# Emptying the finished banks first at a change of tile, in a convolution with two feed-forward layers

## The chip, the cores and the metric

The kernel runs on one core of a Trainium2 chip. The metric is the device time of one execution in microseconds (us). The kernel before takes 2165.09 us (median of three runs, 2159.32 to 2166.94).

## What is computed

The reference, cut to what matters:

```python
def _attn_ref(x, weight):            # x: 4 x 4096 x 192, weight: 8 x 7
    w = softmax(weight)              # seven taps for each of eight groups of 24 channels
    out = np.einsum('hk,bskhg->bshg', w, x_unf)   # causal convolution along the sequence
def _moe_ref(x, w_in, w_out):        # 16384 x 192, 192 x 2048, 2048 x 192
    r = np.maximum(x @ w_in, 0.0)
    return (r * r) @ w_out
def _moe2_ref(x, w_in, w_out):
    h = x @ w_in
    return np.maximum(0.01 * h, h) @ w_out
```

The output is `_moe2_ref(_moe_ref(_attn_ref(x)))`, in float32. A float32 operand is split into a high and a low part in a shorter format (`fp32r`), and a product is the sum of products of parts.

## The kernel before

**Tiles and steps.** The 16384 tokens are cut into 32 tiles of 512 (`TT`). A tile passes through layer 1 (squared ReLU) and layer 2 (leaky ReLU). Behind a start with two pairs of tiles, the tiles follow one by one: layer 1 of an even tile t, layer 1 of t + 1, layer 2 of t, layer 2 of t + 1, and so on (`phases`). These four are called here **1e, 1o, 2e and 2o**, and the four together a round. Each tile takes eight steps (`NP`), and a step handles two blocks of 128 of the 2048 hidden values; 512 steps are written out by one Python loop (`for s in range(NS)`), which sets the order of the instructions on each engine by hand. `tc.manual_schedule()` keeps that order.

**What a step does.** TensorE computes the first product `h` of a step (`g1`, 18 matmuls on halves of the rows, that is nine pairs that run side by side) and, two steps later (`LAG`), the second product (`g2_one`, nine pairs too). Between them, in the step's own turn:

- `act`: ScalarE applies the ReLU to the two `h` tiles into `g` (L576 in layer 1, L578 in layer 2).
- `square` (layer 1 only): one `g` is squared on VectorE (L583), the other on ScalarE (L585).
- `high`: ScalarE casts `g` to `hi` (L603), twice.
- `low`: VectorE subtracts, `lo` = `g` - `hi` (L607), twice.
- `add_low`: VectorE adds the two `lo` into `both` (L619). The second product takes `hi`, `lo` and, for one of its banks, `both`.
- `pieces`: other work that a budget places into the steps: the taps of the convolution for tiles to come (L433, L435, result `acc_a` or `acc_b`), the transposes of the input (L411), the splits of a finished layer 1 tile into the input of layer 2 (L475 on ScalarE, L484 on VectorE), and the transposes and stores of a finished layer 2 tile (L763, L768). At most `many` pieces go into one step, 2 in most.

**The change of tile.** A second product sums over the eight steps of a tile in three banks of PSUM, `M`, `F` and `E` (the tags `o0m`, `o1m`, `o0r`, `o1r` take turns as their names, and the fourth is free for the next tile's first bank). When the last one has been issued, `evac_one` empties the banks with functions that the step calls:

- `early` (ScalarE): L743 and L744 copy the two halves of bank E
- `other` (ScalarE): L747 copies one half of bank F
- `add_rest` (VectorE): L750 adds the other half of F and a copy of E
- `add_main` (VectorE): L753 adds bank M and the copies

The next tile's second product needs E's bank from its first third on, and F's from its second third on. TensorE issues in a step: five pairs of `h`, a third of the second product (three pairs), two pairs of `h`, the second third, two pairs of `h`, the last third. At the change the step of the next tile with p = 1 is the one in which the copies stand; `leaving` holds them, and `alone` says that a single tile is leaving. In the kernel before, `early` stands at the head of that step, `other` and `add_rest` behind the step's activations, its piece and its squares, and `add_main` at its end. The built program makes L750 wait for L747. For a pair of tiles `evac` has six functions (`take`, `shift`, `add`; L835, L840, L844), called at the end of the step.

The first 16 steps follow a written-out table (`ROW`, `play`) and are not touched.

Of the kernel before, what the change touches and what calls it, by code (L numbers as in the profile page):

```python
# [23 lines left out]
LAG = 2  # L24
# [39 lines left out]
def conv_moe_moe2_kernel(  # L64
# [16 lines left out]
    NP = NF // 2  # L81
# [221 lines left out]
    in_pair = {u for z in phases if len(z) == 2 for u in z}  # L303
# [428 lines left out]
    def evac_one(u):  # L732
# [25 lines left out]
        else:  # L758
# [21 lines left out]
            elif t % 2:  # L780
                then.append((700, rest, None, None))
        return (early, other, add_rest, add_main), then

# [18 lines left out]
    def evac_last(u):  # L802

        l, t = u
        (early, other, add_rest, add_main), _ = evac_one(u)
        early()
        other()
        add_rest()
        add_main()
        v = halves(t % 2)  # L810
# [14 lines left out]
    def evac(u):  # L825
# [7 lines left out]
        def take(i):  # L833
            z[i] = ring[:, i, :]
            (nc.vector.tensor_copy if i else nc.scalar.copy)(out=z[i], in_=o[i, "m"])  # L835
# [9 lines left out]

        now = [(0, lambda: take(0)), (690, lambda: take(1))]
        for i in range(2):
            now += [(0, lambda i=i: shift(i)), (690, lambda i=i: add(i))]
        if l == 1:
# [20 lines left out]
    with tc.manual_schedule():  # L870
# [285 lines left out]
        prep_next = 2  # L1156
        late = []
        left_at = -2
        going = begin_g1(0)
        for s in range(NS):  # L1160
# [45 lines left out]
            many = MANY[l - 1] + (l == 1 and s >= 4 * NP or 2 * NP - 4 <= s < 2 * NP) if s > 1 else 4  # L1206
            if left_at == s - 1:
                many = 1
# [3 lines left out]
            if s < 2 * NP:  # L1212
                play(s, A, Z)
                late = [Z]
                if s == 0:
                    split_a((1, 2), third)
                    split_a_lo((1, 2), third)
                continue
            if leaving:
                while leave:  # L1220
                    z = leave.popleft()
                    z[2]()
                    release()
                    budget[0] -= max(z[1], 0)
                while dec and getattr(dec[0][2], "second", False):
                    decode_one()
                if alone:
                    leaving[0]()
            left = [many, 1]
            if u in in_pair:  # L1230
                act(*A)
                if late and late[0] not in hi:
                    high(*late[0])
                if not alone:
                    needed(s, 10000)
                    pieces(s, left)
                while leaving and not alone and dec and getattr(dec[0][2], "second", False):
                    decode_one()
                if l == 1:
                    square(*A, False)  # L1240
                if alone:
                    leaving[1]()
                    leaving[2]()
                    leaving[3]()
                    needed(s, 10000)
                    pieces(s, left)
                if late:
# [5 lines left out]
            else:  # L1253
# [7 lines left out]
                needed(s, 10000)  # L1261
                if not (alone and dec):
                    pieces(s, left, 700)
                if l == 1:
                    square(*Z, vector)
                    square(*A, False)
                if alone:
                    leaving[1]()
                    leaving[2]()
                pieces(s, left)  # L1270
                while leaving and not alone and dec and getattr(dec[0][2], "second", False):
                    decode_one()
                high(*one)
# [3 lines left out]
                if three:  # L1277
                    add_low(u, p)
                if alone:
                    leaving[3]()  # L1280
                    budget[0] -= 1400
            if leaving and not alone:
                for c, fn in leaving:
                    fn()
                    budget[0] -= c
            release()
# [42 lines left out]
```

## Time and profile before

| | |
|---|---|
| median of three runs | 2165.09 us |
| the profiled execution, its own time | 2162.51 us |
| its span, first to last instruction | 2160.8 us |
| mean granted TensorE clock | 0.995 |
| TensorE matmul / weight load busy | 2084.4 / 1974.9 us |
| VectorE / ScalarE busy | 1648.7 / 1478.4 us |

The span is what the trace covers; the execution's own time is 1.7 us longer. PE is TensorE's matmuls, PEld its weight loads, DVE is VectorE, ACT is ScalarE. "idle before" of an instruction is the time its engine stood empty ahead of it, with what ended that time. Matmuls overlap, so busy time of PE is not work at full rate.

### The profile page before, as it was taken

How to read it: one execution, taken by the hardware profiler on the slowest of the kernel's cores; microseconds unless marked ns; L12 is line 12 of the kernel's file. 1: busy time of each engine (PE TensorE's matmuls, PEld its weight loads, DVE VectorE, ACT ScalarE, POOL GpSimd, SP SyncE). 2: the span in 40 equal slices, each digit the busy share in tenths (PEclk: the TensorE clock that was granted, in tenths of full speed). 3: DMA queues.
4: the chain of work that ended last, by engine and by line, in shares of the span. 5: the costliest groups of instructions: out<-in, count | busy, mean ns of one | idle time of the engine just before them, and what ended most of it. 6: DMA issues, size and time to landing. Idle time of an engine off the chain costs nothing.

```text
span 2160.8 us, 47005 instructions
## 1 busy us (share of the span) xinstructions
PE 2084.4 (96%) x18592; PEld 1974.9 (91%) x18592; DVE 1648.7 (76%) x2575; ACT 1478.4 (68%) x2700; POOL 60.1 (3%) x114
## 2 busy tenths in 40 slices
PE   9899999999999999999999999999999999999998
PEld 6789998999999899998999999999998999989997
DVE  8877678787787877778777787877778777787664
ACT  7877567667676666767667676676767667677674
POOL 2201110000000000000000000000000000000000
PEclk9999999999999999999999999999999999999999
DMA  8540131121212112131121211212121121311110
GB/s 191 137 108 21 27 54 26 39 37 45 37 24 46 29 45 40 21 65 26 36 38 32 50 26 38 37 44 38 24 50 26 45 41 21 64 26 35 25 31 16
DMA packets 232677, 95.07 MB, mean 44 GB/s; under 512 B 203208, under 2 KB 218696, under 8 KB 232456
## 3 DMA queue, kind: packets, MB, share of 16 engines
q1 hardware_dynamic: 229288, 88.90, 21.0%
q0 software_dynamic: 1168, 2.75, 0.6%
q8 instruction: 145, 2.38, 0.5%
q14 instruction: 76, 0.62, 0.1%
q10 hardware_dynamic: 2000, 0.42, 0.1%
HBM read 25.19 MB, written 12.58 MB: 17 GB/s over the span
## 4 chain that ended last, share of the span: by engine, by line
PE 65%; DVE 17%; ACT 11%; issue 5%; DMA 1%; SPq 0%; DVEq 0%; ACTq 0%
PE h L544 31%; PE o1m L544 12%; PE o0r L544 11%; PE o1r L544 7%; DVE lo L607 5%; PE o0m L544 4%; ACT hi L603 2%; DVE g L583 2%; DVE acc_b L435 2%; DVE ring L750 2%; ACT g L576 2%; DVE acc_a L435 2%; ACT ring L747 2%; ACT zs L744 2%; ACT g L578 2%
## 5 line engine op out<-in xcount | busy, mean ns | idle before, releaser
L544 PE MATMUL h<-x,w 64*128 64x512 f32 x9216 | 1362.9, 377 | 2.6 <-ACT g L578 1.4
L544 PEld LDWEIGHTS h<-x,w 64*128 64x128 f32 x9216 | 1067.5, 186 | 13.8 <-ACT g L578 1.8
L607 DVE TENSOR_TENSOR lo<-g,hi 128x512 fp32r<-128x512 f32 x1022 | 661.8, 688 | 347.1 <-ACT hi L603 289.7
L603 ACT CAST hi<-g 128x512 fp32r<-128x512 f32 x1020 | 580.9, 619 | 134.5 <-DVE g L583 130.8
L544 PE MATMUL o1m<-hi,w 64*128 64x512 f32 x2044 | 632.6, 385 | 30.5 <-DVE ring L750 28.7
L544 PE MATMUL o0r<-hi,w 64*128 64x512 f32 x1948 | 601.6, 384 | 17.9 <-DVE ring L750 17.9
L578 ACT ACTIVATE g<-h 128x512 f32<-128x512 f32 x512 | 279.6, 595 | 321.3 <-PE h L544 320.5
L544 PEld LDWEIGHTS o1m<-hi,w 64*128 64x128 f32 x2044 | 358.5, 186 | 59.9 <-DVE ring L750 37.7
L544 PEld LDWEIGHTS o0r<-hi,w 64*128 64x128 f32 x1948 | 342.2, 186 | 47.6 <-DVE ring L750 26.2
L544 PE MATMUL o0r<-lo,w 64*128 64x512 f32 (+1 forms) x1022 | 383.5, 378 | 0.4 <-DVE lo L607 0.4
L576 ACT ACTIVATE g<-h 128x512 f32<-128x512 f32 x512 | 278.6, 593 | 139.9 <-PE h L544 138.1
L544 PE MATMUL o1m<-both,w 64*128 64x512 f32 x926 | 352.4, 381 | 8.1 <-DVE both L619 8.1
L619 DVE TENSOR_TENSOR both<-lo 128x512 fp32r<-128x512 f32 x463 | 320.5, 692 | 18.0
L544 PE MATMUL o0m<-hi,w 64*128 64x512 f32 x1088 | 326.9, 380 | 4.4 <-ACT ring L835 3.2
L544 PE MATMUL o1r<-hi,w 64*128 64x512 f32 x1052 | 321.2, 380 | 1.0 <-ACT zs L744 1.0
L544 PE MATMUL o0m<-lo,w 64*128 64x512 f32 x560 | 209.1, 378 | 0.6 <-DVE lo L607 0.5
L544 PEld LDWEIGHTS o0m<-hi,w 64*128 64x128 f32 x1088 | 191.2, 186 | 9.7 <-ACT ring L835 4.0
L544 PE MATMUL o1r<-lo,w 64*128 64x512 f32 (+1 forms) x526 | 198.0, 376 | 0.0
L544 PEld LDWEIGHTS o1m<-both,w 64*128 64x128 f32 x926 | 172.3, 186 | 19.0 <-DVE both L619 16.8
L544 PEld LDWEIGHTS o0r<-lo,w 64*128 64x128 f32 (+1 forms) x1022 | 187.4, 183 | 2.3 <-issue 0.8
L544 PEld LDWEIGHTS o1r<-hi,w 64*128 64x128 f32 x1052 | 186.6, 186 | 2.4 <-ACT zs L744 1.4
L583 DVE TENSOR_TENSOR g<-g 128x512 f32<-128x512 f32 x243 | 165.6, 682 | 20.1 <-ACT g L576 17.4
(136 smaller groups left out, 1337.6 us busy)
## 6 DMA issues: line engine op xcount, KB each, us to landing
x<-x SPq DMA_DIRECT2D x189, 256.0 KB
out_dram<-y SPq DMA_DIRECT2D x186, 64.0 KB
raw_a<-in_x_dram SPq DMA_DIRECT2D x127, 64.0 KB
raw_b<-in_x_dram SPq DMA_DIRECT2D x62, 64.0 KB
lent<-in_moe_w_out_dram SPq DMA_DIRECT2D x13, 256.0 KB
lent<-in_moe_w_in_dram SPq DMA_DIRECT2D x13, 192.0 KB
lent<-in_moe_w_in_dram SPq DMA_DIRECT2D x13, 128.0 KB
lent<-in_moe_w_out_dram SPq DMA_DIRECT2D x13, 128.0 KB
```

What stands on the lines that cost most here:

```text
L435: nc.vector.scalar_tensor_tensor(out=acc[0], in0=src, scalar=w, in1=acc[0], op0=ALU.mult, op1=ALU.add)
L544: return nc.tensor.matmul(out=o.rearrange("p (b a) -> p b a", a=2), lhsT=w, rhs=z.rearrange("p (a b) -> p b a", a=2), start=begin, stop=end_,)
L576: nc.scalar.activation(out=g, in_=hps.pop((u, f)), func=ACTF.Relu)
L578: nc.scalar.activation(out=g, in_=hps.pop((u, f)), func=ACTF.Prelu, alpha=0.01)
L583: nc.vector.tensor_mul(out=g, in0=g, in1=g)
L603: nc.scalar.copy(out=a, in_=gsp[u, f])
L607: nc.vector.tensor_sub(out=b, in0=gsp.pop((u, f)), in1=f32(hi[u, f]))
L619: nc.vector.tensor_add(out=c, in0=f32(lo[u, 2 * p]), in1=f32(lo[u, 2 * p + 1]))
L744: nc.scalar.copy(out=got["s"][v], in_=E[w])
L747: nc.scalar.copy(out=z3[v], in_=F[w])
L750: nc.vector.tensor_add(out=zr[v], in0=F[v], in1=got["s"][v])
```

## The change

For a single tile, the three copies and the addition that frees bank F (`early`, `other`, `add_rest`) are called together at the head of the step; the pending low parts' sum of the step before (`add_low`, if `soon` said that a change follows) comes right behind them, then activations, squares, at most one piece, the casts and subtractions, and at the end `add_main`. For a pair, all six functions go to the head. The step of a change and the one behind it take one piece each at most; other pieces go to later steps.

```diff
--- before.py
+++ after.py
@@ -779,7 +779,7 @@
                 then.append((700, rest_alone, None, None))
             elif t % 2:
                 then.append((700, rest, None, None))
-        return (early, other, add_rest, add_main), then
+        return (early, other, add_rest), [add_main] + then
 
     ys = {}
 
@@ -802,11 +802,11 @@
     def evac_last(u):
 
         l, t = u
-        (early, other, add_rest, add_main), _ = evac_one(u)
+        (early, other, add_rest), then = evac_one(u)
         early()
         other()
         add_rest()
-        add_main()
+        then[0]()
         v = halves(t % 2)
         z, zr = ring[:, 0, :], ring[:, 2, :]
         dmas = [nc.sync, nc.scalar]
@@ -843,9 +843,7 @@
             v = halves(i)
             nc.vector.tensor_add(out=z["r"][v], in0=o[i, "r"][v], in1=z["s"][v])
 
-        now = [(0, lambda: take(0)), (690, lambda: take(1))]
-        for i in range(2):
-            now += [(0, lambda i=i: shift(i)), (690, lambda i=i: add(i))]
+        now = [lambda: take(0), lambda: take(1), lambda: shift(0), lambda: add(0), lambda: shift(1), lambda: add(1)]
         if l == 1:
             then = []
             for i in range(2):
@@ -1154,7 +1152,7 @@
             return [g1(u, p), 9]
 
         prep_next = 2
-        late = []
+        late, pending = [], deque()
         left_at = -2
         going = begin_g1(0)
         for s in range(NS):
@@ -1204,7 +1202,7 @@
             cost = (2100 if vector else 1400) + (700 if three else 0)
             budget[0] = max(min(budget[0] + (SHORT if three else STEP) - cost, STEP), DEBT)
             many = MANY[l - 1] + (l == 1 and s >= 4 * NP or 2 * NP - 4 <= s < 2 * NP) if s > 1 else 4
-            if left_at == s - 1:
+            if left_at == s - 1 or leaving:
                 many = 1
             if leaving:
                 left_at = s
@@ -1216,6 +1214,7 @@
                     split_a((1, 2), third)
                     split_a_lo((1, 2), third)
                 continue
+            soon = s + 1 >= LAG and steps[s + 1 - LAG][1] == NP - 1 and steps[s + 1 - LAG][0] not in in_pair
             if leaving:
                 while leave:
                     z = leave.popleft()
@@ -1224,26 +1223,20 @@
                     budget[0] -= max(z[1], 0)
                 while dec and getattr(dec[0][2], "second", False):
                     decode_one()
-                if alone:
-                    leaving[0]()
+                for fn in leaving:
+                    fn()
+                budget[0] -= 1400
+            while pending:
+                pending.popleft()()
             left = [many, 1]
             if u in in_pair:
                 act(*A)
                 if late and late[0] not in hi:
                     high(*late[0])
-                if not alone:
-                    needed(s, 10000)
-                    pieces(s, left)
-                while leaving and not alone and dec and getattr(dec[0][2], "second", False):
-                    decode_one()
+                needed(s, 10000)
+                pieces(s, left)
                 if l == 1:
                     square(*A, False)
-                if alone:
-                    leaving[1]()
-                    leaving[2]()
-                    leaving[3]()
-                    needed(s, 10000)
-                    pieces(s, left)
                 if late:
                     low(*late.pop())
                 high(*A)
@@ -1259,30 +1252,21 @@
                 act(*one)
                 act(*two)
                 needed(s, 10000)
-                if not (alone and dec):
+                if not leaving:
                     pieces(s, left, 700)
                 if l == 1:
                     square(*Z, vector)
                     square(*A, False)
-                if alone:
-                    leaving[1]()
-                    leaving[2]()
                 pieces(s, left)
-                while leaving and not alone and dec and getattr(dec[0][2], "second", False):
-                    decode_one()
                 high(*one)
                 high(*two)
                 low(*one)
                 low(*two)
                 if three:
-                    add_low(u, p)
-                if alone:
-                    leaving[3]()
-                    budget[0] -= 1400
-            if leaving and not alone:
-                for c, fn in leaving:
-                    fn()
-                    budget[0] -= c
+                    (pending.append if soon else lambda fn: fn())(lambda u=u, p=p: add_low(u, p))
+            if alone:
+                then[0]()
+                then = then[1:]
             release()
             if u in in_pair and l == 1:
                 square(*Z, vector)
```

On **ScalarE**, at a change from layer 2 to an even tile of layer 1 (the one at 1105 us in the trace; `ring` and `zs` are where the banks are copied to). Before:

```order
L603 CAST hi<-g 128x512 x2
L743 COPY ring<-o1m 64x512
L744 COPY zs<-o1m 64x512
L576 ACTIVATE g<-h 128x512 x2
L585 ACTIVATE g<-g 128x512
L747 COPY ring<-o0r 64x512
L603 CAST hi<-g 128x512 x2
```

With the change:

```order
L603 CAST hi<-g 128x512 x2
L743 COPY ring<-o1m 64x512
L744 COPY zs<-o1m 64x512
L747 COPY ring<-o0r 64x512
L576 ACTIVATE g<-h 128x512 x2
L585 ACTIVATE g<-g 128x512
```

The third copy (L747) has moved ahead of the two activations (L576) and the square (L585).

On **VectorE**, at the same change (`both` is the sum of two `lo`, `acc_b` a tap of the convolution, `y` the transposed output). Before:

```order
L607 TENSOR_TENSOR lo<-g,hi 128x512 x2
L619 TENSOR_TENSOR both<-lo 128x512
L435 SCALAR_TENSOR_TENSOR acc_b<-xT_b,taps,acc_b 128x512
L583 TENSOR_TENSOR g<-g 128x512
L750 TENSOR_TENSOR ring<-o0r,zs 64x512
L435 SCALAR_TENSOR_TENSOR acc_b<-xT_b,taps,acc_b 128x512 x2
L607 TENSOR_TENSOR lo<-g,hi 128x512 x2
L619 TENSOR_TENSOR both<-lo 128x512
L753 TENSOR_TENSOR ring<-o1r,ring 128x512
L763 STREAM_TRANSPOSE y<-ring 128x512
```

With the change:

```order
L607 TENSOR_TENSOR lo<-g,hi 128x512 x2
L750 TENSOR_TENSOR ring<-o0r,zs 64x512
L619 TENSOR_TENSOR both<-lo 128x512
L583 TENSOR_TENSOR g<-g 128x512
L435 SCALAR_TENSOR_TENSOR acc_b<-xT_b,taps,acc_b 128x512
L607 TENSOR_TENSOR lo<-g,hi 128x512 x2
L619 TENSOR_TENSOR both<-lo 128x512
L753 TENSOR_TENSOR ring<-o1r,ring 128x512
L763 STREAM_TRANSPOSE y<-ring 128x512
```

The first `both` here is the sum of the step before. It has moved behind the addition L750, the square L583 too; of three taps around the square one is left, behind it.

On **VectorE**, at the next change, from an even to an odd tile of layer 1 (1139 us in the trace). Before:

```order
L619 TENSOR_TENSOR both<-lo 128x512
L435 SCALAR_TENSOR_TENSOR acc_a<-xT_a,taps,acc_a 128x512
L583 TENSOR_TENSOR g<-g 128x512
L750 TENSOR_TENSOR ring<-o1m,zs 64x512
L607 TENSOR_TENSOR lo<-g,hi 128x512 x2
L619 TENSOR_TENSOR both<-lo 128x512
L753 TENSOR_TENSOR ring<-o0m,ring 128x512
L583 TENSOR_TENSOR g<-g 128x512
```

With the change:

```order
L435 SCALAR_TENSOR_TENSOR acc_a<-xT_a,taps,acc_a 128x512
L607 TENSOR_TENSOR lo<-g,hi 128x512 x2
L750 TENSOR_TENSOR ring<-o1m,zs 64x512
L619 TENSOR_TENSOR both<-lo 128x512
L583 TENSOR_TENSOR g<-g 128x512
L607 TENSOR_TENSOR lo<-g,hi 128x512 x2
L619 TENSOR_TENSOR both<-lo 128x512
L753 TENSOR_TENSOR ring<-o0m,ring 128x512
L435 SCALAR_TENSOR_TENSOR acc_a<-xT_a,taps,acc_a 128x512
```

L750 has moved ahead of the pending sum and the square, and a tap has come in behind L753.

## Rows read from the trace of the kernel before

**Rows 1.** Page, part 1: busy time, share of the span, instructions of each engine.

```profile
PE 2084.4 (96%) x18592; PEld 1974.9 (91%) x18592; DVE 1648.7 (76%) x2575; ACT 1478.4 (68%) x2700; POOL 60.1 (3%) x114
```

**Rows 2.** Waits of TensorE over the whole span: total us, times, longest us.

```profile
PE o1m L544 <- DVE ring L750: 28.7, 30, 2.4
PE o0r L544 <- DVE ring L750: 17.9, 28, 1.0
...
PE o0m L544 <- ACT ring L835: 3.2, 2, 2.6
...
PE o1m L544 <- DVE ring L835: 1.8, 2, 1.2
```

**Rows 3.** Stretches: window, length, busy us (x instructions), clock, DMA, GB/s.

```profile
1104.24:1139.13 34.89, 33.30 (x299) 31.32 (x297) 30.91 (x49) 23.97 (x43) 0.00 (x0) 1.00 0.14 17
```

**Rows 4.** Timeline, TensorE: start, us, engine, line, operation, xcount.

```profile
1041.29 1.32 PE L544 MATMUL h<-x,w 64*128 64x512 f32 x10
...
1045.92 1.32 PE L544 MATMUL h<-x,w 64*128 64x512 f32 x10
...
1073.17 1.32 PE L544 MATMUL h<-x,w 64*128 64x512 f32 x10
...
1077.79 1.32 PE L544 MATMUL h<-x,w 64*128 64x512 f32 x10
...
1105.04 1.32 PE L544 MATMUL h<-x,w 64*128 64x512 f32 x10
...
1106.63 0.38 PE L544 MATMUL o1m<-both,w 64*128 64x512 f32 x1
...
1107.20 0.39 PE L544 MATMUL o1m<-hi,w 64*128 64x512 f32 x1
...
1108.56 0.48 PE L544 MATMUL o0r<-hi,w 64*128 64x512 f32 x1 [0.97 <-DVE ring L750]
...
1110.33 1.32 PE L544 MATMUL h<-x,w 64*128 64x512 f32 x10
...
1139.06 1.32 PE L544 MATMUL h<-x,w 64*128 64x512 f32 x10
...
1145.23 1.32 PE L544 MATMUL h<-x,w 64*128 64x512 f32 x10
```

**Rows 5.** Timeline, ScalarE: bank copies at four changes of tile.

```profile
1040.48 0.58 ACT L743 COPY ring<-o1m 64x512 f32<-64x512 f32 x1 [1.42 <-PE o1m L544]
...
1072.36 0.58 ACT L743 COPY ring<-o0r 64x512 f32<-64x512 f32 x1 [0.78 <-PE o0r L544]
...
1104.24 0.58 ACT L743 COPY ring<-o1m 64x512 f32<-64x512 f32 x1 [0.69 <-PE o1m L544]
...
1139.13 0.58 ACT L743 COPY ring<-o0r 64x512 f32<-64x512 f32 x1
```

**Rows 6.** Timeline, VectorE: change of tile at 1105 and the step behind.

```profile
1107.81 0.69 DVE L750 TENSOR_TENSOR ring<-o0r,zs 64x512 f32<-64x512 f32 x1 [1.05 <-ACT ring L747]
1108.54 1.54 DVE L435 SCALAR_TENSOR_TENSOR acc_b<-xT_b,taps,acc_b 128x512 f32<-128x512 f32 x2
...
1113.40 0.65 DVE L583 TENSOR_TENSOR g<-g 128x512 f32<-128x512 f32 x1
```

**Rows 7.** Timeline, VectorE: change of tile at 1139 and the steps behind.

```profile
1134.65 1.30 DVE L607 TENSOR_TENSOR lo<-g,hi 128x512 fp32r<-128x512 f32 x2 [0.68 <-ACT hi L603]
...
1137.25 0.68 DVE L583 TENSOR_TENSOR g<-g 128x512 f32<-128x512 f32 x1
1137.85 0.74 DVE L435 SCALAR_TENSOR_TENSOR acc_a<-xT_a,taps,acc_a 128x512 f32<-128x512 f32 x1
...
1145.85 0.68 DVE L583 TENSOR_TENSOR g<-g 128x512 f32<-128x512 f32 x1
...
1152.45 0.69 DVE L619 TENSOR_TENSOR both<-lo 128x512 fp32r<-128x512 f32 x1
```

**Rows 8.** Timeline, TensorE: the product that takes the sum of 1152.45.

```profile
1154.53 0.38 PE L544 MATMUL o1m<-both,w 64*128 64x512 f32 x1
```

## The prediction, made before the changed kernel was run

> **What bounds the kernel now.** I read the page first, then the waits of TensorE, then the timeline around changes of tile. The page has TensorE at 96% [rows 1], so time can come only from where its products stand still. The list of waits says where: behind the additions that free bank F, 28.7 us in 30 waits and 17.9 us in 28, and at the two changes of pairs 3.2 and 1.8 us [rows 2]. Those figures are only what is left of a pause when the next instruction is already there, so I take the price from the steps. In [rows 4] each run of ten `h` products that starts at 1041.29, 1045.92, ... follows the last second product of a step; I call that moment at a change T. From 1045.92 to 1073.17 are seven undisturbed steps: 27.25 / 7 = 3.89 us each. The steps of the four changes take longer [rows 4]:
>
> - into 2e (T = 1041.29): 4.63, that is 0.74 lost
> - into 2o (1073.17): 4.62, 0.73 lost
> - into 1e (1105.04): 5.29, 1.40 lost; the whole tile to 1139.06 takes 34.02 and loses 2.88
> - into 1o (1139.06): 6.17, 2.28 lost
>
> The sum is 6.6 us a round, some 14 rounds, so 93 us is all that these places hold.
>
> **The change, step by step.** *The three copies.* ScalarE starts L743 at T - 0.81, T - 0.81, T - 0.80 and T + 0.07 (2e, 2o, 1e, 1o) [rows 5]. A copy takes 0.58, and I take 0.60 from start to start. Put behind each other, the third starts 1.20 later and ends 1.78 behind the first: T + 0.97 at three changes, T + 1.85 into 1o. L750 then starts 0.03 later (today 1107.20 + 0.58 to 1107.81, [rows 5, 6], where L747 ends the 1.05 of idle time) and takes 0.69: F is free at T + 1.7, into 1o at T + 2.55. TensorE wants F two pairs of `h` and three of the second product behind T + 1.08; into 1e its first product on F came at 1108.56 and its partner waited from 1107.20, T + 2.16 [rows 4]. So at three changes F is in time and the wait behind L750 goes; into 1o about 0.3 is left.
>
> *The pending sum.* It is late next. Today `both` of the step before is done long before T + 1. Now it stands behind L750 on VectorE: start 0.73 behind L750 (1107.81 to 1108.54, [rows 6]), 0.69 long, so done at T + 2.42. Where the next tile is even (2e, 1e), TensorE wants it in the first third, at T + 1.59 (1106.63, [rows 4]): it now waits 0.88. A pause costs the step some 0.12 more than the delay of the first product: 1107.20 + 0.08 to 1108.56 are 1.28, the step lost 1.40 [rows 4]. So 1.0 is lost into each even tile. Where it is odd (2o, 1o) the sum is wanted a third later, T + 2.16 + 0.5 = T + 2.7: into 2o it is in time.
>
> - into 2e: 1.0 for 0.74, **0.26 slower**, 14 times: +3.6
> - into 2o: 0 for 0.73, 14 times: -10.2
> - into 1e, the step of the change: 1.0 for 1.40
> - into 1o, the same: some 0.7 for 2.28
>
> *What VectorE gives back in 1e and 1o.* The last two would be 2.0 together, but in these tiles VectorE sets the pace. Squares, casts and subtractions form a chain, 3.9 to 4.0 a step: from 1134.65 to 1138.6 the subtractions repeat behind square, casts and pieces [rows 7]. I follow that chain to the last place where it holds TensorE. Into 1e, L750 starts at T + 1.00 and not at T + 2.77 (1107.81, [rows 6]). Behind it stood two taps (1.54, [rows 6]) and then up to the next square 5.59 in all (to 1113.40); now there stand sum and square (0.65 each as starts go) and one tap fewer (0.75): 6.14. The square is 1.2 **earlier**. Two steps later a tap more stands behind the square, +0.75; another one a step later goes into the gap of 0.68 in which VectorE waits for a cast [rows 7] and costs nothing. Into 1o, today's 8.60 from the square at 1137.25 to that at 1145.85 [rows 7] become: 1.88 to L743 (1139.13, [rows 5]), 1.20 + 0.58 + 0.03 to L750, 1.2 for it and the sum, then 4.6 for a square with its wait for the cast (1.37), two subtractions (1.33), sum, L753 and a tap (0.6 to 0.7 each): 9.5, so +0.9. Together the chain is 0.45 **later** than now. The sum of 1152.45 would be ready at 1152.45 + 0.45 + 0.69 + 0.05 = 1153.64; TensorE takes it now at 1154.53 [rows 7, 8]. It can be 0.89 earlier, less 0.12 for the pause: **0.77 won in 1e and 1o together**, not 2.0. Behind that, steps of 1o have no more taps and the chain is faster than TensorE. 13 rounds: -10.0.
>
> *Ends of the program.* The last 1e and 1o have no convolution left; there the 0.4 of 1e and some 0.9 of 1o stay: -1.3. At the two changes of pairs 3.2 + 1.8 are waited [rows 2]; all six functions at the head should save some 3, and the two changes of the early single tiles, one of which has the longest wait of the list (2.4, [rows 2]), some 1.5: -4.5, with ends of -8 and +3, since the order of the weights' decoding moves too and no row prices that.
>
> The activations run 0.6 later in a step of change; the `h` banks they free are wanted only at the end of the next step, so that is nothing, and the cover is almost a step. The pieces that move to other steps cost nothing in layer 2: VectorE has room there; in 1e they are in the chain above. No DMA is added; the stores follow L763 as before. SP and POOL keep their work.
>
> Sum: 3.6 - 10.2 - 10.0 - 1.3 - 4.5 = -22.4. The profiled execution took 2162.5, which is 2.6 under the median of the three runs: **2140 us**. For the range of this case: 1e and 1o between 0 (the chain 0.77 later than worked out) and -1.5 a round, 2o between -0.5 and -0.73, 2e between 0 and +0.5, the ends as said: 2126 to 2154.
>
> **The rivals.** *A, VectorE does not hold the two tiles.* In tile 1e it is busy 30.91 of 34.89 us [rows 3]. If that room can be used, 1e and 1o lose only the 1.0 and some 0.4 at the changes: 5.16 - 1.4 = 3.8 won instead of 0.77. 13 x 3.8 + 6.6 + 5.8 = 62: 2101 us. The Trainium skill, in Perfetto Trace Analysis, Identifying the Most-Contended Engine, says that for VectorE the share of busy time is a fair measure of how near it is to its limit. By that rule there are 11% left, and the tile could shrink from 34.89 to about 31.1. The chain above speaks against it: the room lies in waits of 0.68 and 1.05 [rows 6, 7] that belong to the chain itself.
>
> *B, it gives everything back.* If none of the moved taps finds a gap (three at 0.75 where I count two), the chain is 1.2 later and 1e and 1o win nothing; with nothing from the early part: -6.6, 2156 us, and with a bit more about 2160. For it speaks that VectorE has hardly a gap there; against it the 0.68.
>
> *C, slower: the copies come late everywhere.* My three changes rest on ScalarE being free at T - 0.8. In the step into 1o it is not: the casts end late and L743 starts at T + 0.07 [rows 5]. If the changed order of pieces pushes ScalarE so far back at the others, each 0.1 there costs 0.1 at the pending sum into 2e and 1e, from the first 0.1 on, and into 2o from 0.2 on. With 0.8: 2e loses 1.8 (+1.06), 1e 1.8 (+0.4), 2o 0.7 (as now), 1o wins nothing: +1.5 a round, 13.5 rounds, less 4.5: 2178 us. It would be slower from some 0.5 on. Against it: the first copies waited 1.42, 0.78 and 0.69 for TensorE at these changes [rows 5], so ScalarE had been free that long.
>
> **How the numbers follow.** My case 0.65, A 0.10, B 0.15, C 0.10. A measurement of this kernel can tell some 0.3% (6.5 us) from no change. My own range lies wholly under that, so faster is 0.65 + 0.10 and a little of B: 0.76; the rest of B is the same, 0.14; C is slower, 0.10. The range reaches from my case down a little toward A and up over most of B: 2120 to 2160.
>
> **What would show it.** Right: no waits of TensorE behind L750 at three of four changes, about 0.2 left into 1o; L750 at T + 1.0 and the step into 2o at 3.9; new waits behind `both` (L619) of 0.5 or more at every change into an even tile, with steps of 4.9 there, and more of them within 1e and 1o, so that the list of waits has far more than 20 us of them where bank F had 46. 1e and 1o together take about 66.7 where they took 67.4. Wrong: L743 later than T - 0.5 into 2e, 2o or 1e (C); hardly any waits behind `both` in 1e and 1o (A); the two tiles as long as before (B).

## The result, and the profile after

The changed kernel takes 2126.24 us (median of four runs, 2125.54 to 2129.57) where the kernel before takes 2163.84 in the same comparison: 0.983 of the time, with a 95% interval of 0.981 to 0.985. That is 1.7% faster, clear of the noise, and inside the range of 2120 to 2160; the point, 2140, was 14 us too high. The profiled execution took 2129.57 us (span 2127.9), 32.9 less than that of before.

The page of the changed kernel, busy time of the engines (against [rows 1]) and the shares of the chain that ended last:

```profile
PE 2080.6 (98%) x18592; PEld 1946.0 (91%) x18592; DVE 1641.3 (77%) x2575; ACT 1469.1 (69%) x2700; POOL 61.4 (3%) x114
...
PE 66%; DVE 22%; ACT 7%; issue 4%; DMA 1%; SPq 0%; DVEq 0%; POOL 0%; ACTq 0%
```

TensorE's waits over the whole span (against [rows 2]; total us, times, longest us):

```profile
PE o1m L544 <- DVE both L619: 24.5, 65, 0.5
PE o1r L544 <- DVE lo L607: 6.0, 1, 6.0
PE o1m L544 <- DVE lo L607: 2.8, 2, 2.2
...
PE o1m L544 <- DVE ring L750: 0.5, 1, 0.5
```

Of the 46.6 us behind L750 one wait of 0.5 is left, at 141 us, and the 5.0 at the changes of pairs are gone. In their place stand five waits a round behind the sum `both`, and one of 6.0 behind L607. TensorE's timeline in a regular round (against [rows 4]):

```profile
1024.32 1.31 PE L544 MATMUL h<-x,w 64*128 64x512 f32 x10
...
1029.09 1.24 PE L544 MATMUL h<-x,w 64*128 64x512 f32 x9
...
1056.34 1.32 PE L544 MATMUL h<-x,w 64*128 64x512 f32 x10
...
1060.24 1.32 PE L544 MATMUL h<-x,w 64*128 64x512 f32 x10
...
1087.49 1.32 PE L544 MATMUL h<-x,w 64*128 64x512 f32 x10
...
1089.85 0.48 PE L544 MATMUL o1m<-both,w 64*128 64x512 f32 x1 [0.47 <-DVE both L619]
...
1092.27 1.32 PE L544 MATMUL h<-x,w 64*128 64x512 f32 x10
...
1153.74 1.31 PE L544 MATMUL h<-x,w 64*128 64x512 f32 x10
```

Read as moments T: the step into 2e takes 4.77 (before 4.63), into 2o 3.90 (before 4.62), into 1e 4.78 (before 5.29), and 1e and 1o together, from 1087.49 to 1153.74, take 66.25 (before 67.43). A round is +0.14 - 0.72 - 1.18 = 1.76 us shorter.

The ledger of the two profiled executions, by T of the first and of the last 1e: the first comes at 310.74 instead of 317.03, 6.3 won in the early part (14.9 by the 2250th matmul, 276.43 against 291.28, and 8.6 lost again); the thirteen rounds between them take 1682.5 instead of 1706.2, 23.7 won, 1.8 each; behind the last one 2.9 are won. Together 32.9.

### The profile page after: what moved, and what is told of

The parts are those of the page before. It is cut to its first block, busy times and chain, and to the rows that moved or that the text cites. A ratio compares the mean times of both kernels' runs of the same rounds, so it can differ in the third digit from the quotient of the medians.

```text
span 2127.9 us, 46893 instructions
## 1 busy us (share of the span) xinstructions
PE 2080.6 (98%) x18592; PEld 1946.0 (91%) x18592; DVE 1641.3 (77%) x2575; ACT 1469.1 (69%) x2700; POOL 61.4 (3%) x114
## 4 chain that ended last, share of the span: by engine, by line
PE 66%; DVE 22%; ACT 7%; issue 4%; DMA 1%; SPq 0%; DVEq 0%; POOL 0%; ACTq 0%
PE h L544 32%; PE o1m L544 12%; PE o0r L544 11%; PE o1r L544 7%; DVE lo L607 6%; PE o0m L544 5%; DVE both L619 4%; DVE g L583 4%; ACT hi L603 3%; DVE acc_b L435 1%; DVE acc_a L435 1%; DVE ring L750 1%; ACT ring L743 1%; ACT zs L744 1%; ACT ring L747 1%
## 5 line engine op out<-in xcount | busy, mean ns | idle before, releaser
L544 PEld LDWEIGHTS h<-x,w 64*128 64x128 f32 x9216 | 1038.0, 186 | 23.4 <-ACT g L578 1.3
L607 DVE TENSOR_TENSOR lo<-g,hi 128x512 fp32r<-128x512 f32 x1022 | 661.6, 688 | 325.7 <-ACT hi L603 295.6
L544 PE MATMUL o1m<-hi,w 64*128 64x512 f32 x2044 | 623.3, 382 | 0.5 <-DVE ring L750 0.5
L544 PE MATMUL o0r<-hi,w 64*128 64x512 f32 x1948 | 586.9, 379 | 0.0
L544 PE MATMUL o1m<-both,w 64*128 64x512 f32 x926 | 360.2, 389 | 25.6 <-DVE both L619 24.5
L576 ACT ACTIVATE g<-h 128x512 f32<-128x512 f32 x512 | 277.3, 591 | 60.1 <-PE h L544 59.3
L585 ACT ACTIVATE g<-g 128x512 f32<-128x512 f32 x269 | 169.0, 631 | 7.8
## 6 DMA issues: line engine op xcount, KB each, us to landing
lent<-in_moe_w_in_dram SPq DMA_DIRECT2D x13, 128.0 KB
lent<-in_moe_w_out_dram SPq DMA_DIRECT2D x13, 128.0 KB
```

Source lines behind the costliest of these rows:

```text
L544: return nc.tensor.matmul(out=o.rearrange("p (b a) -> p b a", a=2), lhsT=w, rhs=z.rearrange("p (a b) -> p b a", a=2), start=begin, stop=end_,)
L576: nc.scalar.activation(out=g, in_=hps.pop((u, f)), func=ACTF.Relu)
L585: nc.scalar.activation(out=g, in_=g, func=ACTF.Square)
L607: nc.vector.tensor_sub(out=b, in0=gsp.pop((u, f)), in1=f32(hi[u, f]))
```

## The change into 1e, as the trace shows it

In the kernel before, the third copy into 1e stood behind the step's activations and its square, at T + 2.16:

```profile
1107.20 0.58 ACT L747 COPY ring<-o0r 64x512 f32<-64x512 f32 x1
```

With the change it starts at T + 0.28. ScalarE and VectorE at the change at T = 1087.49 (against [rows 5, 6]):

```profile
1086.69 0.58 ACT L743 COPY ring<-o1m 64x512 f32<-64x512 f32 x1 [0.69 <-PE o1m L544]
1087.28 0.58 ACT L744 COPY zs<-o1m 64x512 f32<-64x512 f32 x1
1087.77 0.58 ACT L747 COPY ring<-o0r 64x512 f32<-64x512 f32 x1
...
1088.38 0.69 DVE L750 TENSOR_TENSOR ring<-o0r,zs 64x512 f32<-64x512 f32 x1 [1.23 <-ACT ring L747]
1089.11 0.69 DVE L619 TENSOR_TENSOR both<-lo 128x512 fp32r<-128x512 f32 x1
1089.71 0.69 DVE L583 TENSOR_TENSOR g<-g 128x512 f32<-128x512 f32 x1
```

L750 stands at the head of VectorE's queue for 1.23 us until L747 is through, and the sum behind it, whose inputs had long been there, is done at 1089.80, T + 2.31. TensorE takes it at 1089.85 (above); in an undisturbed step it would at T + 1.59 [rows 4]. That is 0.77 late, and the step, 4.78 long where an undisturbed one takes 3.89, loses 0.89.

## The experiments

The first three take the change apart. **e1** is the changed kernel with the sum in its own step:

```diff
-                    (pending.append if soon else lambda fn: fn())(lambda u=u, p=p: add_low(u, p))
+                    add_low(u, p)
```

> The changed kernel, with the pending sum of low parts computed at the end of its own step again, ahead of the addition that frees bank F. Theory (the sum's deferral is the cost that the change pays, the early copies and addition are what it wins): VectorE computes the sum in the 0.9 to 1.3 us in which it otherwise stands empty ahead of L750, L750 keeps its start at T + 0.9 to 1.0, the steps into 2e and 1e shorten from 4.78 to 3.9, TensorE's waits behind `both` fall from 24.5 us in 65 to under 8, and in 1e and 1o VectorE's chain is some 1.2 earlier: about 2 us a round, 2126 - 30 = 2096. Rival (the deferral is needed, since the sum ahead of L750 keeps bank F back): waits behind L750 return and the time is 2126 or more.

Measured: 2103.5 us (2100.8 to 2106.6), ratio to before 0.972 [0.9705, 0.9735]. It is 23 us faster than the change. The steps into 2e, 2o and 1e are all clean (3.9), and a round takes 127.8 in the mean and not 129.4. L750 starts at T + 0.88, so the sum ahead of it does not hold bank F back, and the rival is out. The gain is smaller than the theory's 30 us: what remains is in 1e and 1o, where the 13.0 us of waits behind `both` stand (under 8 were expected).

**e2** is the changed kernel with the old rule for the pieces:

```diff
-            if left_at == s - 1 or leaving:
+            if left_at == s - 1:
...
-                if not leaving:
+                if not (alone and dec):
```

> The changed kernel with the rule for other pieces of the kernel before: two or three pieces in the step of a change, one of them ahead of the squares. Theory (VectorE's chain counts every tap once wherever it stands, and only gaps hide one): two taps more in the step into 1e, two fewer behind it and one fewer in 1o, so within 0.4 us a round of the changed kernel, 2120 to 2132. Rival (the early release works only because the step of a change is kept short): the taps ahead of the square make the step into 1e and the two tiles behind it 1 us longer a round, 2140 or more.

Measured: 2144.55 us (2142.5 to 2146.6), ratio 0.9906 [0.989, 0.9923]. That is over what the theory expected and where its rival had it: in the changed kernel the rule that thins out the pieces is worth 18 us. Its waits behind `both` are 29.4 us in 68:

```profile
PE o1m L544 <- DVE both L619: 29.4, 68, 0.6
```

Into 1e, with the old rule, the step of the change takes 4.78, as in the changed kernel; the chain is late two steps further on, and that step takes 5.41 (4.17 in the changed kernel).

**e3** is the kernel before, with only the third copy and L750 moved to the head:

```diff
                 if alone:
                     leaving[0]()
+                    leaving[1]()
+                    leaving[2]()
...
-                if alone:
-                    leaving[1]()
-                    leaving[2]()
```

> The kernel before with one part of the change alone: at a change of a single tile the third copy and the addition that frees F are called at the head of the step; sum, pieces and the changes of pairs as before. Theory: the waits behind L750 (46 us) go nearly all, no waits behind `both` at the changes into 2e and 1e; round by round as e1 (some 3.5 us shorter than before), without what the pairs gave: 2100 to 2112. Rival (sum and pieces have to move with them): 2126 to 2150, with new waits behind L750 or `both`.

Measured: 2111.6 us (2108.6 to 2111.9), ratio 0.9754 [0.9739, 0.9768]. So with the copies first the four versions are 2144.6 (sum deferred, old pieces), 2126.2 (deferred, new: the change), 2111.6 (in place, old), 2103.5 (in place, new). Deferring the sum costs 23 us with the new pieces and some 33 with the old; the one move of L747 and L750 does better than the whole change. The four are not a clean table, since e3 also leaves the changes of pairs as they were. By the profiles, e3 comes to its first 1e at 312.41 and e1 at 304.59, and a round takes 128.0 and 127.8: what e1 has over e3 lies mostly in the early part, and with the sum in place the thinner pieces are worth only some 2 us over the thirteen rounds.

**e4 and e5** leave work out of VectorE's chain, in the changed kernel and in the one before (the same edit):

```diff
         def tap(k):
+            if t >= 4 and 2 <= k <= 5:
+                acc["at"] = now[0]
+                acc["n"] += 1
+                return
```

> The changed kernel without taps 2 to 5 of the convolution from the fifth tile on (the instructions are left out, everything else keeps its place and order), which takes 12 operations of 0.75 us, 9 us a round, off VectorE. Theory (VectorE's chain sets the pace of 1e and 1o): the two tiles shorten from 66.25 to about 63.5, the waits behind `both` inside them go and only those of the changes into 2e and 1e stay (0.5 each): 2126 - 13 x 2.7 = 2091. Rival (VectorE has room, as its busy share says, and the waits come from elsewhere): within 5 us of 2126.

> The kernel before without taps 2 to 5 of the convolution from the fifth tile on, the partner of e4_four_taps_left_out (2104.75). Theory (a step of change in the kernel before loses its time behind L750 whatever VectorE has to do besides): 0.74, 0.73 and 1.4 stay at the changes into 2e, 2o and 1e, the one into 1o falls from 2.28 to about 1.4, since ScalarE is no longer late there, and the waits behind `both` go: 124.5 + 4.3 a round for 131.2, so 2163.8 - 13 x 2.4 = 2132, and the change is worth 27 us without the taps where it is worth 37 with them. Rival (what the change wins is that taps stand elsewhere): without taps the two kernels are within 8 us of each other, 2105 to 2113.

Measured, from one execution each: e4 2104.75, e5 2130.91. Without the taps the change is worth 26 us, and with them 38; e5 is where its theory had it. e4 lies between its theory (2091) and its rival (within 5 us of 2126). The steps within 1e come down, but one of 1o still takes 4.58. So taps are in the chain, and yet leaving out four of seven gives back only 1.9 a round: the amount of VectorE's work was not the whole reason.

**e8** puts L750 ahead of the third copy in e1:

```diff
-        return (early, other, add_rest), [add_main] + then
+        return (early, add_rest, other), [add_main] + then
...
```

> e1_sum_in_place with the order of L747 and L750 turned round: VectorE reads bank F first, ScalarE behind it. VectorE's empty wait ahead of L750 shrinks by 0.6 and the third copy ends 0.7 later, with the activations behind it. Theory (in 1e and 1o the square needs its activation, which now comes at T + 2.3 and not T + 1.6, so the chain is later by some 0.6 at each of the two): 0.5 to 1 us a round slower, 2110 to 2117. Rival (VectorE's empty wait is what the chain loses): 0.5 us a round faster, 2097.

Measured: 2135.67 us (2135.0 to 2139.9), ratio 0.9873 [0.9853, 0.9893]: the direction as expected, but 32 us over e1 where at most 14 were expected. At the change at T = 1088.07 L747 now waits for the addition, with ScalarE's activations queued behind it:

```profile
1089.29 0.58 ACT L747 COPY ring<-o0r 64x512 f32<-64x512 f32 x1 [0.85 <-DVE ring L750]
1089.89 1.09 ACT L576 ACTIVATE g<-h 128x512 f32<-128x512 f32 x2
...
1090.52 0.69 DVE L583 TENSOR_TENSOR g<-g 128x512 f32<-128x512 f32 x1 [1.26 <-ACT g L576]
```

The activations come at T + 1.82; in the changed kernel they came at T + 0.88 (1088.37). The square then waits 1.26, and two steps behind the change a step takes 5.41 (4.62 in e1). The 0.85 at the head of a queue came back as a loss in the chain behind it, larger than the expectation had counted.

**e7** was to hold the optional pieces back in layer 1 of e1 until they are due:

```diff
-                    if q[0][1] >= 0 and budget[0] <= 0 and (q[0][4] if q is dec else q[0][0]) > s:
+                    spent = budget[0] <= 0 or (q is prep and s >= THREE and steps[s][0][0] == 1)
+                    if q[0][1] >= 0 and spent and (q[0][4] if q is dec else q[0][0]) > s:
```

> e1_sum_in_place with one line more: in layer 1 a piece of the convolution is taken only when it is due, not because the budget allows it, so most taps move from 1e to 2e and 2o. Theory (VectorE's chain sets the pace of 1e and 1o, and VectorE has room in layer 2, 23 of 31 us busy): the 3.2 us that 1e and 1o still lose a round in e1 fall to 1.0 to 1.5, 2103.5 - 13 x 1.9 = 2079. Rival (taps in 2o crowd the squares that begin at its end, or the taps become due so late that the next 1e waits for its input): 2100 or more.

Measured: 2281.34 us (2279.5 to 2283.1), ratio 1.0542 [1.0522, 1.0561]: a miss by 200 us, on the side of the rival (pieces that become due too late). From TensorE's waits between 800 and 1000 us, and SP's queue (DMAs issued) there:

```profile
PE h L544 <- DMA x<-x: 9.4, 3, 6.8
```

```profile
875.73 21.27 SPq L797 DMA_DIRECT2D out_dram<-y  x8
897.17 2.78 SPq L453 DMA_DIRECT2D x<-x  x1
```

The last split of the convolution's result (L484) now comes just before the first use, and the DMA that rearranges it (L453) still has to pass SP's queue, where eight stores stand ahead of it. The due times left no room for that, and the run loses some 13 us a round against e1 (140.5 to 127.8; the one step at 894 us takes 18.25, with three waits for L453's transfers and a granted clock that falls to 0.52 between 902 and 906 us); it says nothing on the chain.

**e6** meant to cure the wait of 6.0 by sending every second store of the pair through GpSimd's queue, in e1:

```diff
-                store(y(), i, j, T[i], 32 * j)
+                store(y(), i, j, T[i], 32 * j, nc.gpsimd if j % 2 else None)
...
```

> e1_sum_in_place with every second store of the second pair's output issued by GpSimd's queue instead of SyncE's. In the changed kernel and in e1 TensorE waits 6.0 us once, at 286 us, behind a chain that begins with VectorE waiting 8.5 us for the buffer `y` that those twelve stores read (33 us of issue on one queue). Theory (the issue of the stores holds the buffer): the one wait goes, 2103.5 - 6 = 2097.5. Rival (the other transfers in flight hold it, or the stores on GpSimd take as long): 2103 or more.

Measured: 2117.36 us (2116.6 to 2119.9), ratio 0.9788 [0.9766, 0.981], 14 us slower than e1 where 6 less were expected. The wait behind L607 is gone, and another is there:

```profile
PE o1m L544 <- POOLq L706: 15.4, 1, 15.4
```

```profile
256.38 1.80 POOL L797 DMA_DIRECT2D out_dram<-y  x1 [4.03 <-issue]
260.03 1.79 POOL L797 DMA_DIRECT2D out_dram<-y  x1 [1.85 <-issue]
264.95 1.79 POOL L797 DMA_DIRECT2D out_dram<-y  x1 [3.13 <-issue]
```

L706 is a no-operation on GpSimd by which the halves of TensorE take turns on a bank (`paired`). It stood behind the stores, and TensorE behind it, from 249 to 265 us. Nor was SP done sooner with half of the stores:

```profile
244.58 33.29 SPq L797 DMA_DIRECT2D out_dram<-y  x6
```

Six stores took as long there as twelve do in the changed kernel (33.04, below). So the stores' time in a queue is not a price for each of them, as the expectation took it.

### What limits 1e and 1o

In e1 these two tiles still lost 3.3 us a round. VectorE and then ScalarE in its 1e:

```profile
1082.18 0.65 DVE L583 TENSOR_TENSOR g<-g 128x512 f32<-128x512 f32 x1
1082.75 1.53 DVE L435 SCALAR_TENSOR_TENSOR acc_b<-xT_b,taps,acc_b 128x512 f32<-128x512 f32 x2
1084.19 1.29 DVE L607 TENSOR_TENSOR lo<-g,hi 128x512 fp32r<-128x512 f32 x2
...
1086.79 0.68 DVE L583 TENSOR_TENSOR g<-g 128x512 f32<-128x512 f32 x1
```

```profile
1085.01 0.64 ACT L585 ACTIVATE g<-g 128x512 f32<-128x512 f32 x1
1087.51 1.14 ACT L603 CAST hi<-g 128x512 fp32r<-128x512 f32 x2 [1.86 <-DVE g L583]
1088.55 1.07 ACT L576 ACTIVATE g<-h 128x512 f32<-128x512 f32 x2
```

ScalarE has squared its own half at 1085.65 and then stands 1.86 us, because the first of its two casts is the half that VectorE squares; the casts, and the next step's activations behind them, start only when that square is done, and VectorE's next square needs those activations. That is a loop over both engines. **e9** is e1 and changes nothing but which half comes first, in the casts and in the subtractions:

```diff
+                one, two = A, Z
                 high(*one)
                 high(*two)
                 low(*one)
                 low(*two)
```

> Kernel: e1_sum_in_place, and in the steps of single tiles of layer 1 ScalarE casts first the half that it squared itself and then the one that VectorE squared; VectorE's two subtractions follow in the same order. No instruction is added or left out. In e1 the tiles 1e and 1o still lose 3.3 us a round (steps of 4.62, 4.63, 4.19, 4.27, 4.33, 4.58), and in most of their steps VectorE's first subtraction waits 0.68 for a cast that itself waited 1.1 to 2.0 for VectorE's square. Theory (these waits are links of the chain that sets the pace, so VectorE's 30.4 busy of 33.7 us in 1e leave no room as things are ordered): with another cast in front the wait of 0.68 goes, VectorE works without gaps, 30.4 fit into the 31.1 that TensorE takes, and of 3.3 a round some 2.2 come back; 13 rounds: 29 us, 2075 (2067 to 2088). Rival (VectorE's amount of work sets the pace, the waits are slack that would only move elsewhere): no change, 2098 to 2108.

**e10** is the same edit in the changed kernel, **e12** in the kernel before:

> Kernel: the changed kernel (the pending sum deferred) with the order of casts and subtractions of e9_own_square_cast_first. Theory: the deferral's price at the two even tiles (0.9 each, 1.8 a round) has nothing to do with the square and stays; what the chain costs in 1e and 1o beyond that (66.25 - 62.2 - 0.9 = 3.1 a round) comes back by some 2.2: 2126 - 29 = 2097 (2088 to 2110), and the distance to e9 stays near the 23 us between the changed kernel and e1. Rival (the losses within 1e and 1o come from the deferral, which pushes VectorE's queue back): 2120 to 2130, while e9 gains.

> Kernel: the kernel before, with the order of casts and subtractions of e9_own_square_cast_first and nothing else. The question is the step of the prediction by which VectorE's chain keeps back most of what the change would win in 1e and 1o. As they are, the change is worth 38 us (2164 to 2126). Theory (the chain of square, cast and subtraction hides a part of the change's gain, so with the chain loosened the change must be worth more): in before the pauses behind L750 stay 1.40 into 1e and fall from 2.28 to about 1.4 into 1o (the casts end earlier, so the first copy starts earlier than T + 0.07), the step of 5.01 in 1e loses half of its 1.12; in all 1.7 a round, 13 rounds, 22 us less: 2140 (2130 to 2150), and the change with this order (e10, 2089) is then worth 43 us or more. Rival (the two win the same time, so together they overlap): 2125 or less, and the change would be worth 36 us or less with this order.

Measured: e9 2074.53 us (2073.5 to 2077.0), ratio 0.9596 [0.9582, 0.9611]; e10 2089.08 (2088.5 to 2090.7), 0.9661 [0.9645, 0.9677]; e12 2137.14 (2136.3 to 2138.6), 0.988 [0.9863, 0.9896]. All three fell into the range of the theory, e9 within 1 us and e10 at the low end of its own; that e10 would stay near 23 us behind e9 did not come true (14.6). TensorE's waits in e9, e10 and e12:

```profile
PE o1m L544 <- DVE both L619: 2.4, 10, 0.2
```

```profile
PE o1m L544 <- DVE both L619: 13.2, 28, 0.5
```

```profile
PE o1m L544 <- DVE ring L750: 20.5, 30, 2.4
PE o0r L544 <- DVE ring L750: 17.9, 28, 1.0
...
PE o1m L544 <- DVE both L619: 2.1, 13, 0.2
```

And tile 1e in the changed kernel, in e1 and in e9, from its first copy to that of the next change (length, busy us of PE, PEld, DVE, ACT and POOL, clock, DMA, GB/s; against [rows 3]):

```profile
1086.69:1120.92 34.23, 33.42 (x300) 31.26 (x298) 30.84 (x49) 23.89 (x44) 0.00 (x0) 1.00 0.15 17
```

```profile
1071.00:1104.69 33.69, 33.05 (x298) 31.18 (x297) 30.82 (x49) 23.56 (x44) 0.00 (x0) 1.00 0.15 17
```

```profile
1058.82:1090.93 32.11, 31.87 (x291) 30.54 (x289) 30.55 (x49) 24.89 (x43) 0.00 (x0) 1.00 0.15 18
```

As many instructions of VectorE, 49 with 30.5 to 30.9 us of work, go into 32.11 us as well as into 33.69 and 34.23. From e1 to e9 only the order of the casts and subtractions differs. So the pace was set by the order in which the two engines wait for each other, and not by the amount of VectorE's work alone; that less work helps too, e4 showed. With the loop loosened the change is worth 48 us (2137.1 to 2089.1) where it is worth 38 as things were: the loop held back some 10 us of it. And the deferral costs 14.6 (2089.1 against 2074.5) instead of 23. The step lengths say why: e10 loses 0.89 into 2e, 0.89 into 1e and then 0.26 and 0.07; e9 loses nothing at the changes but 0.32, 0.65 and 0.08 within 1e and into 1o. That is 1.06 a round in favour of e9, some 14 us. The deferral is paid in full at 2e, and most of what it costs into 1e (0.89) comes back within 1e and 1o, where e10 loses 0.33 and e9 1.05; that VectorE catches up in the pause is a reading of these lengths and was not tested by itself.

### The one wait of 6.0

Early in the changed kernel, VectorE, TensorE, and SP's queue:

```profile
284.35 0.71 DVE L763 STREAM_TRANSPOSE y<-ring 128x512 f32<-128x512 f32 x1 [8.51 <-DMA x<-x]
```

```profile
286.30 0.79 PE L544 MATMUL o1r<-lo,w 64*128 64x512 f32 x1 [6.04 <-DVE lo L607]
```

```profile
245.98 33.04 SPq L797 DMA_DIRECT2D out_dram<-y  x12
```

L763 writes the one buffer `y` from which the pair's twelve stores read; they leave SP until 279, and L763 starts 5.3 us behind that. The row puts the wait down to a transfer `x<-x`, which L763 does not touch. That the stores hold the buffer is read from the program and from the kernel before, where the same L763 also starts some 5.2 us behind the last of the twelve and its short wait is put down to a store:

```profile
293.18 0.71 DVE L763 STREAM_TRANSPOSE y<-ring 128x512 f32<-128x512 f32 x1 [1.67 <-DMA out_dram<-y]
```

**e11** puts other work ahead of that L763, in e9:

```diff
-            then.append((700, main, None, None))
+            k = now[0]
+            then.append((700, main, (lambda: now[0] >= k + 5) if t == 2 else None, None))
```

> Kernel: e9_own_square_cast_first, and the output transpose (L763) of tile 2, the first that needs the buffer which the pair's twelve stores still read, comes some three steps later on VectorE. In the changed kernel and in e1 this one instruction stood 8.5 us at the head of VectorE, until the last of the twelve stores (2.75 us each on SP) was through, and TensorE lost 6.0. Theory: with other work ahead of it the wait is covered: 6.0 less, so e9 less 4 to 6, and no wait over 1 us of TensorE behind L607 at 280 us. Rival (the stores and the loads behind them on SP are then later, and something else waits for those): no gain, within 2 of e9.

Measured: 2069.73 us (2066.9 to 2071.5), ratio 0.9571 [0.9557, 0.9586], 4.8 less than e9, as expected, and the wait is gone. That shows what the wait cost, not which transfer ends it. It is the fastest version: 56 us less than the changed kernel.

## Why the prediction was right, point by point

- *The waits behind L750 are the price, and moving the copies pays it.* Right. L743 starts at T - 0.81, T - 0.80, T - 0.80 and T + 0.08 (2e, 2o, 1e, 1o), so C did not happen. L750 was forecast at T + 1.0 and came at T + 0.89; no wait behind it is left in a round, into 1o neither (0.2 to 0.3 was forecast). e3 shows that this move alone brings 52 us.
- *The pending sum is late next.* Right in place and kind, a little over in size: TensorE was forecast to wait 0.88 and the even steps to lose 1.0; it was 0.77 and 0.89. The term that was off is the 0.60 from start to start of the copies: the third starts 1.08 behind the first, not 1.20. The restart of 0.12 held. So 2e is +0.14 instead of +0.26, and 2o -0.72 for -0.73. The waits behind `both` sum to 24.5 us, where far more than 20 was given as the sign. e1 confirms the place: without the deferral the steps into 2e and 1e are clean.
- *VectorE gives most of 1e and 1o back.* Right in kind: 1.18 a round won, 0.77 forecast, and not the 3.8 of rival A. The chain was worked out 0.4 too late: the sum that in the kernel before starts at 1152.45, 47.41 behind T of 1e, starts at 1134.97 with the change, 47.48 behind it, so 0.07 later and not 0.45; part of that is the copies' 0.12. But the reason was named too loosely. The text put the room in "waits of 0.68 and 1.05 [rows 6, 7] that belong to the chain itself", and took the chain for a given. e9 shows that the link is the order of the casts, which can be turned round at no cost.
- *Rival A and the rule on the busy share.* In Perfetto Trace Analysis, Identifying the Most-Contended Engine, the Trainium skill takes the share of busy time of VectorE for a fair measure of how near it is to its limit. The trace agrees that there was room: in e9 the tile takes 32.11 us with VectorE 95% busy, where the changed kernel has 34.23 and 90%. But the share does not tell how to reach the room: the moved copies brought the tile from 34.89 only to 34.23, and rival A's 3.8 a round did not come.
- *The early part.* -4.5 was forecast with ends of -8 and +3, and -6.3 measured, but as the difference of two numbers that no step of the prediction had; that the total is near is luck. The changes there won 14.9: by the count of matmuls the changed kernel is 10.0 ahead at the 1900th (238.52 against 248.47) and 14.0 at the 2000th (249.37 against 263.38), and between the two lies one change of a pair, at which before waited only 0.54 and 1.18 behind L835. Of the rest some 1.6 is the clock, shown below (an estimate: 13 matmuls start in the 3 us from 254 where 28 start in 3 us at full clock). Then the wait of 6.04, with the low clock behind it, took 8.6 back. The tiles that came earlier ran into the pair's stores: L763 stands at the head of VectorE 15.7 us earlier than in the kernel before (275.84 against 291.51), the twelve stores begin only 8.9 earlier (245.98 against 254.91), and its wait is 6.8 longer. And e11, which covers that wait, comes to its first 1e 5.1 us before e9 (300.61 against 305.66). The prediction had no term for that wait.
- *The late end* gave 2.9 instead of 1.3.
- *The sum.* -22.4 against the -32.9 of the profiled executions (-37.6 by the medians): 13 rounds at 0.53 more (0.41 in 1e and 1o, 0.12 in 2e) are 7, the early part 1.8, the end 1.6. Each term but the early part's two halves had its place and sign; most were sized on the slow side, and the median, 2126.24, lies at the very edge of the 2126 to 2154 that the case was given.
- *Rival B* (all given back) held for the variant e2 better than for the change: with the pieces of before in place it keeps only 19 of its 38 us. That the thinner pieces matter so much beside the deferral was not in the sum, which gave the taps a place in 1e but no price of their own.

## What to carry to other kernels

When a stall is removed by moving work to the head of a queue, ask what that head then waits for and who stands behind it: here a ready sum behind an addition that waits 1.23 us cost 23 us, while the same sum left in its own place costs these steps nothing. When an engine has room by its busy time and the tile will not shrink, look for two engines that wait for each other in turn within a step, and let each of them first do what it can do alone. Test the parts of a change singly; its best part may beat the whole.

## What the runs showed of the hardware

- A row of stores leaves its queue slowly. Of the twelve on SP (33.04 us) the first took 0.80 us, the second 2.04 and the others 2.90 to 3.01 each, while the DMA engines moved 22 to 23 GB/s; a store of 64 KB takes 3.0 us at 22. Eight in a row took 21.27. It is no fixed price of a store: in e6, with six on each of two queues, those on SP took 5.89 in the median and up to 9.41, and those on GpSimd 1.79 to 2.53, with gaps of 1.9 to 4.0 between the last ones. What sets the pace of such a row the runs do not show. Anything else in that queue, a rearranging DMA (a wait of 6.8 in e7) or a no-operation that TensorE waits for (15.4 in e6), is late by what stands ahead of it.
- An early wait cost more than its length: with waits of 0.54 and 1.18 the kernel before lost 4.1 us to the changed one. At the second change of pairs in the kernel before the granted clock is 1.00 up to 254 us, TensorE busy for 1.49 of the last 3 us, and 0.51 in the 3 us behind that, all of them busy (columns as in [rows 3]):

```profile
251.00:254.00 3.00, 1.49 (x11) 1.15 (x12) 2.94 (x5) 2.06 (x4) 0.00 (x0) 1.00 0.01 3
254.00:257.00 3.00, 3.00 (x17) 3.00 (x16) 0.87 (x2) 0.53 (x2) 0.79 (x3) 0.51 0.04 6
```

In the changed kernel the same change has no wait, and the clock stays at 1.00. Behind its own wait of 6.04 the clock falls too:

```profile
280.00:284.00 4.00, 0.25 (x3) 0.00 (x0) 0.00 (x0) 0.16 (x1) 0.00 (x0) 1.00 0.49 89
...
286.00:288.00 2.00, 1.70 (x8) 1.43 (x10) 1.93 (x4) 0.00 (x0) 0.00 (x0) 0.50 0.14 21
288.00:291.00 3.00, 3.00 (x16) 2.34 (x16) 2.96 (x5) 0.89 (x2) 1.49 (x3) 0.50 0.20 22
291.00:295.00 4.00, 4.00 (x38) 3.45 (x38) 3.24 (x6) 2.08 (x5) 0.80 (x3) 0.94 0.21 22
```

0.50 is the lower of the two levels, 1.2 GHz: 14 matmuls start in the 3 us from 288 where 28 start in the 3 us from 243, at 1.00 (the rows count also those that began earlier and still run). The short waits in the regular rounds, 0.2 to 1.0, leave the clock at 1.00 ([rows 3] and the window of 1e above).
